# Two more of the seven output sums get a second level of seven-for-eight products, and activations, sums and their results move into rings of one tile

## The chip, the cores and the metric

The kernel runs on one core of a Trainium2 chip. The metric is device time in microseconds (us) of one execution; the kernel before takes 1898.63 us (median of 3 runs, 1898.58 to 1900.76).

## The reference, cut to what matters

```python
def _attn_ref(x):                       # x: (8, 3008, 256) float32
    X = np.fft.fft(x, axis=1)
    X = np.fft.fft(X, axis=2)
    return X.real.astype(np.float32)

def _moe_ref(x, w_in, w_out):           # x: (24064, 256), w_in: (256, 2048), w_out: (2048, 256)
    h = x @ w_in
    g = h * (1.0 / (1.0 + np.exp(-1.702 * h)))
    return (g @ w_out).astype(np.float32)
```

The real part of a two-dimensional Fourier transform of eight sequences, then a layer with 2048 hidden features, a sigmoid-GELU, and a second matrix back to 256 columns. Everything is float32.

## The kernel before, in words

**Stages.** For each of the eight sequences (`b`) the transform over the 3008 positions is done in two stages, 47 x 64 (`fold1`, `mix1`, a round trip through DRAM, `stage2`). The transform over the 256 columns is folded into the first weight matrix (`fold_w`). Position k and its mirror position share the folded operands, so each hidden feature is computed once as a sum (`begin`, two halves `cs`) and the mirrored value is `2*g - x` read backwards (`backward`).

**Steps.** The main loop runs over 384 steps `t`: 8 sequences, 3 blocks `blk`, 2 halves `hh` of 256 (once per sequence 226) positions, and 8 steps `p`, each with two tiles of 128 hidden features. Eight steps with one `(b, blk, hh)` are a group: there are 48, and each gives one pair of output blocks. In a step the activations form a 2 x 2 block matrix, A11 and A12 (forward positions, two feature tiles) and A21 and A22 (mirrored positions).

**First level.** The output of a group is a sum over its eight steps of products of that 2 x 2 matrix with a 2 x 2 matrix of weight tiles. Seven block products with sums of blocks (S1 to S4 of activations, T1 to T4 of weights in `wt`) replace the eight. Each of the seven has its own accumulator in PSUM (`po0` to `po4`, one bank each). A block product is two matmuls of 128 x 64 weights over 256 columns that run side by side in the two halves of the array (`halves`). `product(t)` issues them three steps (`LAG = 3`) after the activations of step t were begun.

**Second level.** For two of the seven, those with A12 and A22 themselves, the operands of two neighbouring steps are cut once more into 2 x 2 and multiplied with seven products of half the width (`small_products`, k = 1 to 7, each one matmul of 64 rows per operand, 128 columns wide). `deeper` makes the four sums that they need, `small_weights` the weight differences. All groups do so but the first (eight plain products) and the last (one level): 46 groups, `deep(t)`.

**End of a group.** `combine` copies the first accumulator out of PSUM (ACT, line 694) and adds others onto it (DVE, line 700). `combine_small`, one step later, puts the small products together (DVE, line 723), `swap` exchanges two halves of the partitions (ACT, lines 731 to 733), `combine_last` adds both levels, transposes and stores.

**Order.** All engines' orders are written out by hand by the loop at the end (a manual schedule); the tile framework adds the waits on semaphores. Within a step PE gets `begin(t, 1)`, part of `product(t-3)`, `begin(t+1)`, the rest of the product, then the small products: k = 1, 2, 4, 7 of the pair that ends in step t-3 in one step, k = 5, 6, 3 in the next. ACT gets `forward` (line 552), `doubled` (545), `activate_back` (559), `middle` (533). DVE gets `backward` (506), two sums of `sums` (574, 575), `deeper` (592). POOL gets the other two sums (571, 572). At the first step of a new group (`t - 3` divisible by 8, called the opening step below) `cut` is 0: PE does `begin(t, 1)` and `begin(t+1)` first, then the product, then the last small products of the old group.

Of the kernel before, what the change touches and what calls it, by code (L numbers as in the profile page):

```python
# [111 lines left out]
def kernel(ctx: ExitStack, tc, x, w_in, w_out, tab1, tab2, out):  # L112
# [12 lines left out]
    hp = ctx.enter_context(tc.tile_pool(name="hp", bufs=4, space=SB))  # L125
    sp = ctx.enter_context(tc.tile_pool(name="sp", bufs=2, space=SB))
# [20 lines left out]

    def mat(w, jj, rows):

        return w[rows, jj * NM:jj * NM + 64]  # L150
# [3 lines left out]
    def bank(name, tag=None):  # L154
        if tag is None:
            tag = spare.pop(0)
            spare.append(tag)
        return psp.tile([128, 512], F32, tag=tag, name=name)
# [198 lines left out]
    def load_in(n, eng):  # L357
        t = raw["in", n] = cv.tile([128, 1024, 2], U32, tag="raw", bufs=3, name="raw")
        eng.dma_start(out=t[:].rearrange("p (i f) w -> p i (f w)", i=2),
                      in_=w_in[:, n * 512:(n + 1) * 512].bitcast(U32).rearrange("(i p) f -> p i f", p=128))  # L360

    def load_out(n, eng):
        t = raw["out", n] = cv.tile([128, 1024, 2], U32, tag="raw", bufs=3, name="raw")
# [5 lines left out]
    def prepare(key):  # L369


        g = sp.tile([128, 1024], F32, tag="s", bufs=3, name="g")
        m = cv.tile([128, 1024], F32, tag="m", bufs=2, name="m")
        r = cv.tile([128, 1024], U32, tag="r", bufs=2, name="r")
        pre[key] = g, m, r
# [28 lines left out]
    def high(key, lo=0, n=1024):  # L404
# [3 lines left out]
        if lo == 0:  # L408
            made_a[key] = cv.tile([128, 1024], U32, tag="a", name="a")
# [57 lines left out]
    vb, ht, st, rt, xb, gt, pot = {}, {}, {}, {}, {}, {}, {}  # L467
    held = []
# [30 lines left out]
    def reversed_sum(t, x, y, op):  # L499

        n, h = width(t), ht[t]
        full, rest = divmod(n, RUN)
        for at, blocks, m in ((0, full, RUN), (full * RUN, 1, rest)):
            if m:
                ins = [free(z[:], at, [256, 2], [RUN, blocks], [1, m]) for z in (x, y)]
                nc.vector.tensor_tensor(free(h[:], 512 + at + m - 1, [256, 2], [RUN, blocks], [-1, m]), *ins, op=op)  # L506

    def rows(t):
# [4 lines left out]
        h = ht[t] = hp.tile([128, 2, 2, 256], F32, tag="h", name="h")  # L513
        dif = sp.tile([128, 512], F32, tag="dif", name="dif")
# [5 lines left out]
        reversed_sum(t, pa, dif, ALU.add)  # L520
# [21 lines left out]
    def doubled(t):  # L542
        n = width(t)
        g = gt[t] = sp.tile([128, 512], F32, tag="dif" if t % 2 else "v", name="g")
        nc.scalar.activation(two(g[:], n), two(xb[t][:], n), ACTF.Copy, scale=2.0)  # L545

    def forward(t):
        n = width(t)
        if t % 2 == 0:
            pot["h"] = cv.tile([128, 2, 2, 2, 256], F32, tag="raw", bufs=3, name="h")  # L550
        h = ht[t] = pot["h"][:, t % 2]
        nc.scalar.activation(two(h[:], n), two(xb[t][:], n), ACTF.Gelu_apprx_sigmoid)  # L552

    def backward(t):
        reversed_sum(t, gt.pop(t), xb.pop(t), ALU.subtract)

    def activate_back(t):
        g = free(ht[t][:], 512, [256, 2], [1, width(t)])
        nc.scalar.activation(g, g, ACTF.Gelu_apprx_sigmoid)  # L559

    def sums(t, eng):
# [3 lines left out]
        h, n = ht[t], width(t)  # L565
        a11, a12, a21, a22 = h[:, 0, 0, :n], h[:, 0, 1, :n], h[:, 1, 0, :n], h[:, 1, 1, :n]
        if eng is nc.gpsimd:
            st[t] = held[2] if t % 4 == 3 else sp.tile([128, 4, 256], F32, tag="s", bufs=3, name="s")
        s1, s2, s3, s4 = (st[t][:, q, :n] for q in range(4))
        if eng is nc.gpsimd:  # L570
            eng.tensor_tensor(s1, a21, a22, op=ALU.add)  # L571
            eng.tensor_tensor(s3, a11, a21, op=ALU.subtract)  # L572
        else:
            eng.tensor_tensor(s2, s1, a11, op=ALU.subtract)  # L574
            eng.tensor_tensor(s4, a12, s2, op=ALU.subtract)  # L575
# [4 lines left out]

    def deeper(t, part):
# [3 lines left out]
        x0, x1, w = ht[t - 1], ht[t], width(t) // 2  # L585
        if part == 0:
            rt[t] = cv.tile([128, 4, 2, 128], F32, tag="r", bufs=2, name="r")
        s1, s2, s3, s4 = (free(rt[t][:], 256 * q, [128, 2], [1, w]) for q in range(4))
        a11, a12, a21, a22 = (free(x[:], 256 + at, [512, 2], [1, w]) for at in (0, w) for x in (x0, x1))
        for out, i0, i1, how in (((s3, a11, a21, ALU.subtract), (s1, a21, a22, ALU.add)),  # L590
                                 ((s2, s1, a11, ALU.subtract), (s4, a12, s2, ALU.subtract)))[part]:
            nc.vector.tensor_tensor(out, i0, i1, op=how)  # L592

    SUBS = {1: (4, 2), 2: (3, 0), 3: (4, 0), 4: (4, 1), 5: (3, 2), 6: (3, 1), 7: (3, 3)}

    def sub(k):
        q, at = SUBS[k]
        return pot[q][:, at * 128:(at + 1) * 128]

    def small_products(t, ks):  # L600
# [4 lines left out]
        if 1 in ks and p == 0:  # L605
            for q in (3, 4):
                pot[q] = bank(f"po{q}", f"o{q}")
        x0, x1, r = ht[t - 1], ht[t], rt[t]
        for k in ks:
            for side in range(2):  # L610
                y0, y1 = (wo[:, p + i, 2, :] if side == 0 else wt[:, p + i, 3, :] for i in range(2))
                made = held[p // 4][:, p // 2 % 2, :, side]
                fwd = {1: (x0, 0), 2: (x1, 0), 4: (x1, w)}
                rhs = (free(fwd[k][0][:], 256 + 512 * side + fwd[k][1], [1, w]) if k in fwd
                       else r[:, {3: 3, 5: 0, 6: 1, 7: 2}[k], side, :w])
                lhs = {1: y0[:, 0:64], 2: y1[:, 0:64], 3: y0[:, 0:0], 4: made[:, 3], 5: made[:, 0], 6: made[:, 1],
                       7: made[:, 2]}[k]
                if k == 3:
                    lhs = y1[:, 64:128]
                nc.tensor.matmul(sub(k)[64 * side:64 * side + 64, :w], lhsT=lhs, rhs=rhs,  # L620
                                 start=(p == 0 and k in (1, 2)), stop=(p == NP - 2), skip_group_check=True)
        if 3 in ks:
            del rt[t]

    def small_weights(n):

        def y(i, at):
            return free(wot[:], (2 * n + i) * 4 * H + 2 * H + at, [NF // 2 * 4 * H + H, 2], [1, 64])

        b11, b12, b21, b22 = y(0, 0), y(0, 64), y(1, 0), y(1, 64)  # L630
        t1, t2, t3, t4 = (held[n // 2][:, n % 2, q] for q in range(4))
        for out, i0, i1 in (t1, b12, b11), (t2, b22, t1), (t3, b22, b12), (t4, b21, t2):
            nc.gpsimd.tensor_tensor(out, i0, i1, op=ALU.subtract)  # L633

    def product(t, lo, hi):

        p, n = steps[t][3], width(t)
        if lo == 0 and p == 0:
            for q in range(2 if t < NP else 3):
                pot[q] = bank(f"po{q}", f"o{q}")  # L640
            if t >= NP and not deep(t):
                pot[5] = bank("po5", "b2" if deep(t - 1) else "o3")
        h = ht[t]
        if t < NP:

            plan = [(half, dh, wo[:, p, 2 * f + dh, :], h[:, half, f, :n])
                    for half in range(2) for dh in range(2) for f in range(2)]
        else:
            s = st[t]
            plan = [(0, 0, wo[:, p, 0, :], h[:, 0, 0, :n]), (0, 1, wt[:, p, 1, :], s[:, 1, :n]),  # L650
                    (1, 0, wt[:, p, 2, :], s[:, 2, :n]), (1, 1, wt[:, p, 0, :], s[:, 0, :n]),
                    (2, 0, wo[:, p, 3, :], s[:, 3, :n])]
# [352 lines left out]
```

## Time and profile before

| | |
|---|---|
| median of 3 runs | 1898.63 us |
| the profiled execution | 1898.94 us, of which the span is 1897.2 us |
| PE (TensorE) busy | 1879.8 us, 99% of the span |
| PEld (weight loads beside the matmuls) | 1364.9 us, 72% |
| DVE / ACT / POOL busy | 1210.5 / 1117.5 / 786.7 us, 64% / 59% / 41% |
| granted TensorE clock | 0.999 |
| DMA | 104.95 MB, 55 GB/s on average |

The profile shows each float32 matmul as two records, so a block product of two matmuls is four records. Records overlap: a product's time is read from the start of one group of records to the start of the next, not from the length of a record.

### The profile page before, as it was taken

Reading aid. Unit: us, or ns where it says so; the run is one execution under the profiler, and the core shown is the slowest. Engines: PE = TensorE matmul, PEld = TensorE weight load, DVE = VectorE, ACT = ScalarE, POOL = GpSimd, SP = SyncE. Lnnn points to the kernel's source line nnn. Section 1 sums busy time; section 2 is a strip of 40 time slices with the busy share of each in tenths; the row PEclk is TensorE's granted clock in tenths of the full one; section 3 lists DMA queues with packets and bytes.
Section 4 is the critical chain, followed back from the end, with each engine's and each line's share of the span. In section 5 each row is a group of like instructions: output and inputs, shape, how many; then the busy total and the mean of one; then the engine's idle time right before and its main releaser. Section 6 shows DMA issues by size and latency. Waiting matters only on the chain.

```text
span 1897.2 us, 51367 instructions
## 1 busy us (share of the span) xinstructions
PE 1879.8 (99%) x21392; PEld 1364.9 (72%) x21392; DVE 1210.5 (64%) x2635; ACT 1117.5 (59%) x2248; POOL 786.7 (41%) x1074
## 2 busy tenths in 40 slices
PE   9999999999999999999999999999999999999998
PEld 6576789777776777777777677777777767777775
DVE  7666556665676556766667556665665766666654
ACT  6656655665556556565565555656655566556553
POOL 4585324633245333462235533365333643223332
PEclk9999999999999999999999999999999999999999
DMA  8732451236221452316413173132720232212201
GB/s 286 165 50 17 102 72 15 48 56 116 18 27 40 77 93 18 51 23 109 57 14 62 22 124 34 24 51 47 114 26 17 18 50 51 24 14 17 29 13 23
DMA packets 145400, 104.95 MB, mean 55 GB/s; under 512 B 104914, under 2 KB 127986, under 8 KB 143984
## 3 DMA queue, kind: packets, MB, share of 16 engines
q1 hardware_dynamic: 143952, 101.14, 32.6%
q8 instruction: 169, 2.77, 0.6%
q10 hardware_dynamic: 1216, 0.52, 0.1%
q14 instruction: 63, 0.52, 0.1%
HBM read 58.38 MB, written 48.01 MB: 56 GB/s over the span
## 4 chain that ended last, share of the span: by engine, by line
PE 93%; POOL 3%; ACT 1%; DVE 1%; DMA 1%; issue 1%; SPq 0%; POOLq 0%; DVEq 0%
PE po L481 42%; PE x L481 33%; PE po L620 14%; PE ps L232 2%; PE ps L334 1%; DMA raw<-in_moe_w_in_dram 1%; POOL wo L444 1%; PE psw L450 1%; ACT xt L235 0%; DMA wo<-in_tab_dram 0%; POOL held L633 0%; POOL wst L426 0%; ACT x L533 0%; POOL s L572 0%; DVE m L412 0%
## 5 line engine op out<-in xcount | busy, mean ns | idle before, releaser
L481 PE MATMUL x<-pq,wcs 128*64 128x256 f32 (+1 forms) x6016 | 765.7, 377 | 1.0 <-ACT x L533 0.2
L506 DVE TENSOR_TENSOR h<-g,x 128x512 f32<-128x512 f32 (+2 forms) x440 | 257.7, 598 | 535.2 <-ACT h L552 534.8
L481 PE MATMUL po<-s,wo 128*64 128x256 f32 (+1 forms) x4512 | 568.6, 375 | 1.3 <-issue 1.3
L481 PEld LDWEIGHTS x<-pq,wcs 128*64 128x64 f32 x6016 | 420.2, 137 | 175.1 <-ACT x L533 18.6
L571 POOL TENSOR_TENSOR s<-h 128x256 f32<-128x256 f32 (+1 forms) x282 | 206.4, 732 | 790.4 <-ACT h L559 771.8
L481 PEld LDWEIGHTS po<-s,wo 128*64 128x64 f32 x4512 | 332.0, 137 | 148.4 <-issue 1.7
L545 ACT ACTIVATE g<-x 128x512 f32<-128x512 f32 (+1 forms) x376 | 222.0, 590 | 341.3 <-PE x L481 340.1
L552 ACT ACTIVATE h<-x 128x512 f32<-128x512 f32 (+1 forms) x376 | 221.4, 589 | 273.2 <-PE x L481 267.8
L533 ACT ACTIVATE x<-nb,af 128x256 f32<-128x256 f32 (+1 forms) x752 | 352.9, 469 | 13.2 <-DVE pq L340 1.0
L481 PE MATMUL po<-h,wo 128*64 128x256 f32 (+1 forms) x1824 | 262.0, 376 | 0.0
L559 ACT ACTIVATE h<-h 128x512 f32<-128x512 f32 (+1 forms) x376 | 231.3, 615 | 32.9 <-DVE h L506 31.7
L572 POOL TENSOR_TENSOR s<-h 128x256 f32<-128x256 f32 (+1 forms) x282 | 205.9, 730 | 0.0
L481 PE MATMUL po<-held,wo 128*64 128x256 f32 (+1 forms) x1504 | 192.4, 375 | 0.0
L571 POOL TENSOR_TENSOR held<-h 128x256 f32<-128x256 f32 (+1 forms) x94 | 76.4, 812 | 257.0 <-ACT h L559 243.5
L620 PE MATMUL po<-r,held 128*64 128x128 f32 (+1 forms) x2208 | 182.9, 270 | 0.0
L481 PEld LDWEIGHTS po<-h,wo 128*64 128x64 f32 x1824 | 133.8, 137 | 60.0
L592 DVE TENSOR_TENSOR r<-h 128x256 f32<-128x256 f32 (+1 forms) x368 | 165.5, 491 | 0.0
L620 PEld LDWEIGHTS po<-r,held 128*64 128x64 f32 x2208 | 141.0, 137 | 23.8
L481 PEld LDWEIGHTS po<-held,wo 128*64 128x64 f32 x1504 | 110.8, 137 | 48.7
L574 DVE TENSOR_TENSOR s<-s,h 128x256 f32<-128x256 f32 (+1 forms) x282 | 127.7, 453 | 0.0
L575 DVE TENSOR_TENSOR s<-h,s 128x256 f32<-128x256 f32 (+1 forms) x282 | 121.0, 429 | 9.6
L620 PE MATMUL po<-h,wo 128*64 128x128 f32 (+1 forms) x1472 | 111.0, 270 | 0.0
(108 smaller groups left out, 1674.4 us busy)
## 6 DMA issues: line engine op xcount, KB each, us to landing
out_dram<-os SPq DMA_DIRECT2D x284, 64.0 KB
Td<-xt SPq DMA_DIRECT2D x14, 768.0 KB
t<-Td SPq DMA_DIRECT2D x7, 1536.0 KB
xt<-in_x_dram SPq DMA_DIRECT2D x14, 512.0 KB
xt<-Xr SPq DMA_DIRECT2D x14, 512.0 KB
nb<-pq SPq DMA_DIRECT2D x23, 256.0 KB
out_dram<-os SPq DMA_DIRECT2D x96, 56.0 KB
Xr<-in_x_dram SPq DMA_DIRECT2D x7, 752.0 KB
```

The source lines that it names most:

```text
L481: nc.tensor.matmul(out[c0:c0 + 64], lhsT=lhs[:, c0:c0 + 64], rhs=rhs, skip_group_check=True, **how)
L506: nc.vector.tensor_tensor(free(h[:], 512 + at + m - 1, [256, 2], [RUN, blocks], [-1, m]), *ins, op=op)
L533: nc.scalar.activation(x[:, i * 256:i * 256 + n], nbt[b, blk][:, hh * 256:hh * 256 + n], ACTF.Copy, scale=af1[:, f:f + 1])
L545: nc.scalar.activation(two(g[:], n), two(xb[t][:], n), ACTF.Copy, scale=2.0)
L552: nc.scalar.activation(two(h[:], n), two(xb[t][:], n), ACTF.Gelu_apprx_sigmoid)
L559: nc.scalar.activation(g, g, ACTF.Gelu_apprx_sigmoid)
L571: eng.tensor_tensor(s1, a21, a22, op=ALU.add)
L572: eng.tensor_tensor(s3, a11, a21, op=ALU.subtract)
L574: eng.tensor_tensor(s2, s1, a11, op=ALU.subtract)
L575: eng.tensor_tensor(s4, a12, s2, op=ALU.subtract)
L592: nc.vector.tensor_tensor(out, i0, i1, op=how)
L620: nc.tensor.matmul(sub(k)[64 * side:64 * side + 64, :w], lhsT=lhs, rhs=rhs, start=(p == 0 and k in (1, 2)), stop=(p == NP - 2), skip_group ...
```

## The change

Four of the seven output sums now go through the second level: A12 and A22 as before, and S4 and S1. Three stay at the first level (A11, S2, S3). The 46 deep groups therefore issue three block products per step instead of five, and per pair of steps 28 small matmuls (four operands, seven products) instead of 14.

So that one DVE operation can serve four operands, the eight blocks of a step lie in one tile `big`: A11, A21, S3, S2 in a ring of four steps (LEFT), and A12, S4, A22, S1 in a ring of three pairs of steps (RIGHT). `deeper` makes its four sums with one operation of 4 x 128 columns each, three of them in one step and the fourth in the next; before, each operation was 2 x 128 wide. `sums` on DVE runs once per pair of steps, 2 x 256 wide, instead of once per step. The rings of the weight preparation (`raw`, `h`, `r`, `m`, `s`, `a`) are places in the same tile.

In PSUM the five accumulator banks become one tile `acc` of 5 x 512 columns. The three plain sums lie in columns 0 to 767, the small products k = 1 in 768 to 1023, the others in 1024 to 2559.

Order: at the opening step PE does the old group's k = 5, 6, 3 right after `begin(t, 1)`, then `begin(t+1)` and the new group's product. In other steps k = 5, 6, 3 stand ahead of the product's last part. `combine_small` stands ahead of the sums, and `combine_last` and the transposes are spread over three steps. `small_weights` moves from POOL (16 operations) to DVE (32, for four operands). In the prologue the load of the last quarter of `w_in` is issued after the second read of `Td`, which moves ahead of it, and `high(out0)` moves up.

```diff
-    hp = ctx.enter_context(tc.tile_pool(name="hp", bufs=4, space=SB))
+    acc = psp.tile([128, 5 * 512], F32, tag="acc", name="acc")
+    big = cv.tile([128, 19 * 1024], F32, tag="big", name="big")
...
+        if tag[0] == "o":
+            return acc[:, int(tag[1]) * 512:(int(tag[1]) + 1) * 512]
...
+    LEFT, RIGHT, MADE, SUM, RES, OUT = 0, 4096, 10240, 14336, 16384, 18432
+    A11, A21, S3, S2 = range(4)
+    A12, S4, A22, S1 = range(4)
...
     def sums(t, eng):
...
+        if t % 2 == 0:
+            return
+        a11, s2 = (free(big[:], at_left(t - 1, q), [1024, 2], [1, n]) for q in (A11, S2))
+        a12, s4, s1 = (free(big[:], at_right(t - 1, q), [1024, 2], [1, n]) for q in (A12, S4, S1))
+        eng.tensor_tensor(s2, s1, a11, op=ALU.subtract)
+        eng.tensor_tensor(s4, a12, s2, op=ALU.subtract)
...
+    def raws(t, half):
+        return free(big[:], at_right(t, 0) + half * (width(t) // 2), [256, 4], [1, width(t) // 2])
+    def made_sum(q, w):
+        return free(big[:], SUM + 512 * q, [128, 4], [1, w])
     def deeper(t, part):
...
-        for out, i0, i1, how in (((s3, a11, a21, ALU.subtract), (s1, a21, a22, ALU.add)),
-                                 ((s2, s1, a11, ALU.subtract), (s4, a12, s2, ALU.subtract)))[part]:
+        s1, s2, s3, s4 = (made_sum(q, width(t) // 2) for q in range(4))
+        a11, a12, a21, a22 = (raws(k, half) for half in range(2) for k in (t - 1, t))
+        for out, i0, i1, how in (((s3, a11, a21, ALU.subtract), (s1, a21, a22, ALU.add), (s2, s1, a11, ALU.subtract)),
+                                 ((s4, a12, s2, ALU.subtract),))[part]:
...
+    SPOT = {2: 0, 6: 1, 5: 2, 7: 3, 3: 4, 4: 5}
+    def spot(pair_, k):
+        return 768 + 128 * pair_ if k == 1 else 1024 + 768 * pair_ + 128 * SPOT[k]
+    def both(k, *dims):
+        return free(acc[:], spot(0, k), [spot(1, k) - spot(0, k), 2], *dims)
     def small_products(t, ks):
...
+            for pr in range(2):
+                for side in range(2):
+                    op_ = 2 * pr + side
+                    weights, q = ((wo, 2), (wo, 3), (wt, 3), (wt, 0))[op_]
...
     def product(t, lo, hi):
...
-            plan = [(0, 0, wo[:, p, 0, :], h[:, 0, 0, :n]), (0, 1, wt[:, p, 1, :], s[:, 1, :n]),
-                    (1, 0, wt[:, p, 2, :], s[:, 2, :n]), (1, 1, wt[:, p, 0, :], s[:, 0, :n]),
-                    (2, 0, wo[:, p, 3, :], s[:, 3, :n])]
+            plan = [(0, 0, wo[:, p, 0, :], left(t, A11, n)), (0, 1, wt[:, p, 1, :], left(t, S2, n)),
+                    (1, 0, wt[:, p, 2, :], left(t, S3, n))]
...
     def combine(t):
...
+        nc.scalar.copy(c11, acc[:, 0:n])
+        nc.vector.tensor_tensor(c12, c11, acc[:, 256:256 + n], op=ALU.add)
+        nc.vector.tensor_tensor(c21, c12, acc[:, 512:512 + n], op=ALU.add)
         if deep(t):
+            nc.scalar.copy(free(big[:], RES + 1024 + 384, [512, 2], [1, w]), both(1, [1, w]))
+            return
...
     def combine_small(t):
...
+        for out, i0, i1 in ((res(0, 1024), res(1024 + 384, 0), both(2, [128, 2], [1, w])),
+                            (res(1024 + 128, 128), res(1024, 0), both(5, [128, 2], [1, w])),
+                            (res(256, w - 256), res(1024 + 128, 128), both(3, [128, 2], [1, w])),
+                            (res(256 + w), res(1024 + 256), both(5, [1, w]))):
             nc.vector.tensor_tensor(out, i0, i1, op=ALU.add)
...
+            opening = (t - LAG) % NP == 0 and t >= NP + LAG
+            one, other = (t - LAG, (1, 2, 4, 7)), (t - LAG - 1, (5, 6, 3))
+            if opening:
+                small_products(*other)
+            cut = 0 if opening and not after else 3 if after else 2
             product(t - LAG, 0, cut)
...
+            if not opening:
+                small_products(other[0], other[1][after:])
+            product(t - LAG, cut, 6 if t - LAG == last else None)
+            small_products(one[0], one[1][after:])
             swap(t - LAG - 2)
...
+            combine_small(t - LAG - 1)
...
+            sums(t - 1, nc.vector)
             deeper(t - 2, 0)
             deeper(t - 3, 1)
```

In the built program, engine by engine, each wait names the semaphore count that it waits for, and so the instruction that ends it. Around the end of each of the 46 deep groups it has these waits. The copy of c11 (ACT) waits for the last small matmul of the group's last step (k = 7). The adds c12 and c21 (DVE) follow it, and the copy of the k = 1 results (ACT) waits for c21. The first k = 5 matmul of the opening step (PE) waits for that copy. The first operation of `combine_small` (DVE) waits for the last matmul of the new group's first product, and the first matmul of the new group's second product (PE) waits for the last operation of `combine_small`. In the last of the 46 it is the seventh product of the opening step that waits so.

## The prediction

> **What bounds the kernel now.** I read the page's parts 1, 2 and 4 first.
>
> ```profile
> span 1897.2 us, 51367 instructions
> PE 1879.8 (99%) x21392; PEld 1364.9 (72%) x21392; DVE 1210.5 (64%) x2635; ACT 1117.5 (59%) x2248; POOL 786.7 (41%) x1074
> PEclk9999999999999999999999999999999999999999
> PE 93%; POOL 3%; ACT 1%; DVE 1%; DMA 1%; issue 1%; SPq 0%; POOLq 0%; DVEq 0%
> ```
>
> PE is busy in every slice at full clock, and the chain of waits is 93% PE. Matmul time taken off PE comes off the total, and any wait that PE gets is added in full: nothing lies beside it. So I read the timeline around one group's end, where the new accumulators are opened. The opening step starts at 986.45 us. PE, ACT and DVE (start us, length us, engine, line, operation; idle time before it in brackets):
>
> ```profile
> 986.23 0.39 PE L620 MATMUL po<-r,held 128*64 128x128 f32 x4
> 986.45 1.90 PE L481 MATMUL x<-pq,wcs 128*64 128x256 f32 x16
> 986.49 0.36 ACT L694 COPY u<-po 128x256 f32<-128x256 f32 x1
> 986.89 0.95 DVE L700 TENSOR_TENSOR u<-u,po 128x256 f32<-128x256 f32 x2 [1.15 <-ACT u L694]
> 987.53 0.60 ACT L552 ACTIVATE h<-x 128x512 f32<-128x512 f32 x1 [0.52 <-PE x L481]
> 987.87 0.69 DVE L700 TENSOR_TENSOR c<-u,po 128x512 f32<-128x512 f32 x1
> 988.18 0.60 PE L481 MATMUL po<-h,wo 128*64 128x256 f32 x4
> 988.61 1.90 PE L481 MATMUL po<-s,wo 128*64 128x256 f32 x16
> 988.66 0.42 DVE L700 TENSOR_TENSOR c<-c,po 128x256 f32<-128x256 f32 x1
> 990.34 0.61 PE L620 MATMUL po<-r,held 128*64 128x128 f32 x8
> 990.77 0.39 PE L620 MATMUL po<-r,wo 128*64 128x128 f32 x4
> 990.99 1.03 PE L481 MATMUL x<-pq,wcs 128*64 128x256 f32 x8
> 991.60 1.58 DVE L723 TENSOR_TENSOR held<-held,po 128x256 f32<-128x256 f32 x4
> 991.86 0.60 PE L481 MATMUL po<-h,wo 128*64 128x256 f32 x4
> 992.13 0.60 ACT L552 ACTIVATE h<-x 128x512 f32<-128x512 f32 x1 [0.92 <-PE x L481]
> ```
>
> The reader is to see three things. Starts give the prices on PE: four records of 256 columns (one block product) take 988.61 - 988.18 = 0.43 us, eight records of 128 columns 990.77 - 990.34 = 0.43, so a pair of small matmuls costs 0.22, and `begin` 0.87 (990.99 to 991.86). PE has no gap at the group's end. And the copy (986.49) starts before the last small matmuls have ended (986.23 + 0.39 = 986.62), so it doesn't wait for them: in this kernel each accumulator bank is a tile of its own, and `combine` runs beside PE.
>
> **Part 1: matmuls.** Per pair of steps, two operands leave the first level: 2 x 2 block products of 0.433 (12 records from 1002.88 to 1004.18 are three products in 1.30) go, 4 x 0.433 = 1.73 us; 14 small matmuls come, 7 x 0.2175 = 1.52. The gain is 0.21 us. At width 226, `begin` takes 0.76 (1009.49 to 1010.25), a product 0.38 and a small pair, by half, 0.19: gain 0.19. 46 deep groups have 184 pairs, 32 of them (8 sequences x 4) 226 wide: 152 x 0.21 + 32 x 0.19 = 38.0 us less. It is all on the path. Weight loads double in number for these products, but at 128 columns the old ones already keep exactly half the time of 256, so loads do not limit them.
>
> **Part 2: the first new wait.** `acc` is one tile now, and the built program orders every reader and writer of it one after the other, whatever columns they touch. Take T as the start of an opening step. The copy of c11 waits for the last k = 7 matmul, then the chain runs through DVE and ACT back to PE's first k = 5 matmul. Row by row: PE to ACT 0.27 (`begin` issued by 991.86, ACT L552 starts 992.13), with rounding 0.28; copy 0.36; to DVE 0.04 (986.85 to 986.89); two dependent adds 0.98 (986.89 to 987.87); to ACT 0.03 (DVE's `backward` ends 989.68, ACT's L559 starts 989.71); copy of the k = 1 results, now 2 x 128 columns, 0.36; to PE 0.05 (ACT's L533 ends 1017.92, PE's `begin` starts 1017.97). That is T + 2.1 less rounding, 2.07 with T + 0.28 as the start of the copy. PE's cover is `begin(t, 1)`, 0.87. Exposed: 1.20 us, 46 times: 55.2 us. Bounds: 0.98 if the two adds follow at DVE's undependent spacing (0.34 + 0.42), 1.5 if `middle` (0.98 us on ACT just ahead of the copy, ended about 986.55) is 0.3 late. ACT's `forward` is queued behind the second copy, 0.9 us later than now; behind it `backward` and POOL's sums, whose results PE wants three steps later.
>
> **Part 3: the second new wait.** `combine_small` waits for the new group's first product, and PE's next product waits for `combine_small`. Counted from the end of that product: PE to DVE 0.28 (as for ACT); three operations of 512 columns and one of 256, each but the last needing the one before: the row at 987.87 to 988.66 gives 0.79 for 512 dependent from PSUM, `combine_last` to transpose (995.29 to 996.01) 0.72; I take 0.75, so 2.25 + 0.42; to PE 0.14 (in the chain DVE ends 79.42, PE starts 79.56). Sum 3.09. Cover: `begin(t+1, 1)`, 0.87. Exposed 2.22. In 14 of the 46, a `mix1` stands there too (seven sequences, two each): the chain gives line 232 1.6% of the span for 28 of them, 1.08 us; the timeline at 124.01 to 124.81 gives 0.80; I take 1.0, exposed 1.22. The last of the 46 has no `begin` between: 3.09. Together 31 x 2.22 + 14 x 1.22 + 3.1 = 89.0 us. Bounds: 1.77 with undependent spacing (0.60 per 512), which makes 68; 2.8 if POOL beside it slows DVE by the fifth that line 592's mean (509 ns) stands over its median (417), which makes 116.
>
> **Part 4: costed at nothing.** DVE per pair of steps: now eight operations of 0.42 at lines 574, 575 and 592, 3.4 us; then six of 0.69 (the 128x512 row), 4.1. The 184 x 0.7 = 129 us lie in the 535 us in which line 506 waits for ACT. The longer work after an opening (`combine_small`, three `deeper`, `backward`) ends S2 at about T + 12 us where PE wants it at about T + 14; with that cover gone it is rival C. ACT's three swaps (0.40 to 0.59, the 128x512 copy row) and copy add 0.7 us per group, beside PE. Prologue: POOL loses 16 operations of line 633 (about 7.5 us) just ahead of the one larger PE gap below, a gain of at most 1.8; DVE gets 32 of them at 0.28 (its 128x128 row), 9 us over four steps, and the `w_in` quarter loads later, behind a read of `Td` on SP's queue; its first user is step 2's weight preparation. A loss of 3 at most, by PE's gaps there (0.2 to 0.6 us each). I take zero. POOL's S1 and S3 keep their number and size.
>
> The one gap of the old main loop that resembles the new ones, and the clock around it:
>
> ```profile
> 124.01 0.44 PE L232 MATMUL ps<-xt,w 47*64 47x256 f32 x3 [1.78 <-POOL xt L208]
> 122.00:126.00 4.00, 2.22 (x28) 1.28 (x24) 0.69 (x1) 1.03 (x3) 3.92 (x7) 1.00 0.00 0
> ```
>
> The granted clock (the 1.00 after the five engines) stays full over a gap of 1.78 us, so I keep full-clock prices.
>
> A rule against the change: the Trainium skill, "TensorE: Matmul & The Clock Gate", section "What's actually happening", has PE fall to half clock after an idle window of about 3.4 us. The gaps of 1.2 and 2.2 us stay under it; if it struck at each second wait and held for one window, 46 x 1.7 = 78 us would be added, about 2083. A rule for it: "PSUM — Partial Sum Buffer", section "PSUM bank collisions raise a hardware error", asks for waits by bank (or bank and quadrant), not by address; the copy at 986.49 beside matmuls into another bank agrees. By that rule neither wait of parts 2 and 3 is needed, and the sum is 1861; the built program has both, so I go by the program.
>
> **Sum.** The profiled execution took 1898.94 us, 0.3 over the median. 1898.9 - 38.0 + 55.2 + 89.0 = 2005.1 us: slower by 5.6%.
>
> **Rivals.** A: the waits end early enough to be hidden. Place: the two waits at the opening; price 144 us less, 1861 us, faster by 2%. For it: PE has no gap there now. Against: the two chains contain eight operations whose rows exist, and 0.87 us of cover. It decides where both together fall under 38.0 / 46 = 0.83 us per group. B: one of the two is hidden, for instance because work that I don't see stands between on PE: 1916 to 1950. Against: the order on PE is fixed and has only `begin` there. C: the gaps spread. DVE's backlog makes S2 late, or a cold clock follows: up to 1 us more per group, 46 to 80 us, 2050 to 2085. For it: only about 2 us of slack in S2; against: line 506's idle time. D: the change doesn't do what it says, the small matmuls costing more than half: excluded by the 0.43 of eight records.
>
> **Numbers.** Forecast 0.83, A 0.06, B 0.05, C 0.06. The forecast's own bounds: 1898.9 - 38.0 + 46 x 0.98 + 68 - 1.8 = 1972, and 1898.9 - 38.0 + 69 + 116 + 3 = 2049. The range 1968 to 2046 leaves out A, B and C. A measurement tells about 0.2% (4 us) from no change. Faster 0.06, same 0.01 (between A and B), slower 0.93.
>
> **What would show it.** PE busy near 1842 us in a span near 2003. Among the waits, PE for ACT's copy of the k = 1 results 46 times, 1.2 us each, and PE for DVE's `combine_small` 46 times, about 2 us each; PE without gaps between openings; clock 1.0. If there is no gap at the openings, parts 2 and 3 are wrong. If gaps come in each step, it is DVE or the `big` tile (rival C). A saving in PE's busy time other than 38 us would make part 1 wrong.

## The result and the profile after

The changed kernel takes 2033.42 us (median of 4 runs, 2031.64 to 2034.38), the kernel before 1899.64 (4 runs, 1898.58 to 1900.76): a ratio of 1.070, 95% interval 1.069 to 1.072. The forecast was 2005.0 with a range of 1968 to 2046. The profiled execution took 2034.38 us, 135.4 more than the one before. From the page of the changed kernel, parts 1, 2 and 4:

```profile
span 2032.6 us, 55416 instructions
PE 1881.3 (93%) x23600; PEld 1409.7 (69%) x23600; DVE 1493.0 (73%) x2245; ACT 1154.4 (57%) x2248; POOL 934.2 (46%) x1058
...
PEclk9899999999999999999999999999999999999999
...
PE 83%; DVE 9%; ACT 6%; issue 1%; DMA 1%; POOL 0%; SPq 0%; ACTq 0%; DVEq 0%; POOLq 0%
```

PE was busy in 99% of the span and is now busy in 93%. The chain that ended last, 93% PE before, now runs through DVE for 9% and through ACT for 6%: PE waits for them. In these slices the clock is full but for the beginning. The view of the waits of PE (line waited at, and by whose work the wait ended: us in total, times, longest):

```profile
PE acc L493 <- DVE big L758: 61.2, 44, 1.8
PE acc L657 <- ACT big L731: 45.8, 46, 2.0
PE acc L493 <- DVE dif L549: 5.1, 2, 2.8
```

The first two are the two waits that the prediction's parts 2 and 3 priced; line 758 is `combine_small`, line 731 the copy of the k = 1 results. These totals count idle time after the modelled ends of the matmuls; what a wait adds is read from starts. The timeline at one opening step (start us, length us; idle time in brackets):

```profile
1026.14 1.03 PE L493 MATMUL x<-pq,wcs 128*64 128x256 f32 x8
1026.36 0.37 ACT L726 COPY big<-acc 128x256 f32<-128x256 f32 x1
1026.76 0.42 DVE L727 TENSOR_TENSOR big<-big,acc 128x256 f32<-128x256 f32 x1 [0.93 <-ACT big L726]
1027.22 0.42 DVE L728 TENSOR_TENSOR big<-big,acc 128x256 f32<-128x256 f32 x1
1027.67 0.37 ACT L731 COPY big<-acc 128x256 f32<-128x256 f32 x1 [0.94 <-DVE big L728]
1028.10 1.09 PE L657 MATMUL acc<-big 128*64 128x128 f32 x16 [0.92 <-ACT big L731]
...
1031.62 1.03 PE L493 MATMUL x<-pq,wcs 128*64 128x256 f32 x8
1031.83 2.46 DVE L758 TENSOR_TENSOR big<-big,acc 128x512 f32<-128x512 f32 x4 [2.57 <-PE acc L493]
...
1034.35 1.08 PE L493 MATMUL acc<-big,wo 128*64 128x256 f32 x8 [1.70 <-DVE big L758]
```

`begin` keeps PE for 0.86 us (eight records of 107.9 ns). The first one, from 1026.14, would be followed at 1027.00; the small matmuls start at 1028.10, so 1.10 us are exposed. They wait for copy, add, add, copy, one after the other on ACT and DVE, as the prediction chained them. The second `begin`, from 1031.62, covers to 1032.48, and the next product starts at 1034.35: 1.87 us exposed, behind the four operations of `combine_small`.

The third wait above is none of the openings. The start of ACT's first `combine` copy marks the end of the first group with a second level (called the first group below): 138.46 us in the kernel before (first line), 169.98 after (second line).

```profile
138.46 0.34 ACT L694 COPY u<-po 128x226 f32<-128x226 f32 x1
169.98 0.34 ACT L726 COPY big<-acc 128x226 f32<-128x226 f32 x1
```

Thus 31.5 of the 135.4 us come before the main loop has properly begun. From the last such copy to the end are 8.7 us, before 10.2. Between the first and the last one lie 1748.5 us before and 1853.9 after: 105.3 more for 46 groups. The window from 40 to 60 us of this beginning (its length, busy us of the five engines with their instructions, granted clock, DMA share, GB/s), first before the change, then after:

```profile
40.00:60.00 20.00, 19.18 (x140) 11.15 (x138) 17.87 (x25) 16.60 (x24) 10.65 (x7) 1.00 1.01 348
40.00:60.00 20.00, 15.10 (x65) 7.71 (x63) 10.19 (x15) 11.59 (x17) 6.37 (x6) 0.74 0.73 251
```

The clock was 0.74 and not 1.00, and PE had 65 matmul records there, against 140 before. Its timeline there:

```profile
48.29 1.97 PE L493 MATMUL acc<-pq,wcs 128*64 128x256 f32 x8 [2.27 <-DVE dif L549]
...
60.19 3.22 PE L493 MATMUL acc<-pq,wcs 128*64 128x256 f32 x16 [2.81 <-DVE dif L549]
```

These are `begin`-like products of the prologue, into `acc`: `bank()` hands pieces of the one tile to the prologue too. PE waits for DVE to finish reading the last piece, and the eight records take the time from 48.29 to 50.02, 1.73 us, twice the 0.86 of the main loop: half clock.

### The profile page after: what moved, and what is told of

Read it like the earlier page. It is cut to its first block, busy times and chain, and to the rows that moved or that the text cites. A ratio compares the mean times of both kernels' runs of the same rounds, so it can differ in the third digit from the quotient of the medians.

```text
span 2032.6 us, 55416 instructions
## 1 busy us (share of the span) xinstructions
PE 1881.3 (93%) x23600; PEld 1409.7 (69%) x23600; DVE 1493.0 (73%) x2245; ACT 1154.4 (57%) x2248; POOL 934.2 (46%) x1058
## 4 chain that ended last, share of the span: by engine, by line
PE 83%; DVE 9%; ACT 6%; issue 1%; DMA 1%; POOL 0%; SPq 0%; ACTq 0%; DVEq 0%; POOLq 0%
PE x L493 27%; PE acc L657 26%; PE acc L493 25%; DVE big L758 5%; PE ps L346 1%; DVE big L728 1%; DVE big L727 1%; ACT big L731 1%; PE ps L244 1%; ACT x L564 1%; ACT xt L247 1%; ACT big L726 1%; ACT big L579 1%; DVE big L623 1%; DVE big L602 0%
## 5 line engine op out<-in xcount | busy, mean ns | idle before, releaser
L594 POOL TENSOR_TENSOR big<-big 128x256 f32<-128x256 f32 (+1 forms) x376 | 353.1, 939 | 1005.5 <-ACT big L586 770.6
L493 PE MATMUL acc<-big,wo 128*64 128x256 f32 (+1 forms) x4832 | 631.0, 377 | 66.3 <-DVE big L758 61.2
L623 DVE TENSOR_TENSOR big<-big 128x512 f32<-128x512 f32 (+1 forms) x736 | 609.5, 844 | 34.6 <-PE acc L657 19.8
L493 PEld LDWEIGHTS acc<-big,wo 128*64 128x64 f32 x4832 | 340.7, 137 | 231.9 <-DVE big L758 81.0
L537 DVE TENSOR_TENSOR big<-g,x 128x512 f32<-128x512 f32 (+2 forms) x440 | 255.4, 592 | 239.5 <-ACT big L579 238.6
L657 PE MATMUL acc<-big 128*64 128x128 f32 (+1 forms) x5888 | 385.8, 272 | 47.4 <-ACT big L731 45.8
L657 PEld LDWEIGHTS acc<-big 128*64 128x64 f32 x5888 | 334.1, 137 | 90.5 <-ACT big L731 66.4
L579 ACT ACTIVATE big<-x 128x512 f32<-128x512 f32 (+1 forms) x376 | 221.4, 589 | 216.7 <-PE x L493 182.7
L595 POOL TENSOR_TENSOR big<-big 128x256 f32<-128x256 f32 (+1 forms) x376 | 341.5, 908 | 0.0
L657 PE MATMUL acc<-big,wo 128*64 128x128 f32 (+1 forms) x4416 | 303.9, 271 | 0.0
L657 PEld LDWEIGHTS acc<-big,wo 128*64 128x64 f32 x4416 | 259.4, 137 | 28.1
L586 ACT ACTIVATE big<-big 128x512 f32<-128x512 f32 (+1 forms) x376 | 231.8, 616 | 30.3 <-DVE big L537 28.9
L602 DVE TENSOR_TENSOR big<-big 128x512 f32<-128x512 f32 (+1 forms) x188 | 140.2, 746 | 6.5
L601 DVE TENSOR_TENSOR big<-big 128x512 f32<-128x512 f32 (+1 forms) x188 | 131.8, 701 | 1.5 <-POOL big L594 1.5
```

The lines of the kernel that those rows point to most:

```text
L493: nc.tensor.matmul(out[c0:c0 + 64], lhsT=lhs[:, c0:c0 + 64], rhs=rhs, skip_group_check=True, **how)
L537: nc.vector.tensor_tensor(free(out, at + m - 1, [by, 2], [RUN, blocks], [-1, m]), *ins, op=op)
L579: nc.scalar.activation(front(t), two(xb[t][:], width(t)), ACTF.Gelu_apprx_sigmoid)
L586: nc.scalar.activation(back(t), back(t), ACTF.Gelu_apprx_sigmoid)
L594: eng.tensor_tensor(right(t, S1, n), left(t, A21, n), right(t, A22, n), op=ALU.add)
L595: eng.tensor_tensor(left(t, S3, n), left(t, A11, n), left(t, A21, n), op=ALU.subtract)
```

## The experiments

My theory after the result had three parts. (1) The tile `acc` as such makes the waits, by joining five banks into one thing to be ordered, in the openings and in the prologue alike. (2) The waits of the openings add to PE's time in full. (3) Without them the matmuls give their 38 us. The rivals: the second level's longer DVE and ACT work makes PE late in any case; the prologue is slower because of its other edits (moved loads, weight differences on DVE). Each experiment kernel computes the whole result.

**The prologue alone.** Five separate bank tiles until step `t = NP + LAG`, the joined tile from there on:

```diff
-    acc = psp.tile([128, 5 * 512], F32, tag="acc", name="acc")
+    acc = None
+    old = early_banks.enter_context(tc.tile_pool(name="old", bufs=1, space=PS))
...
+        if tag[0] == "o" and acc is None:
+            return old.tile([128, 512], F32, tag=tag, name=name)
...
+        if t == NP + LAG:
+            early_banks.close()
+            acc = psq.tile([128, 5 * 512], F32, tag="acc", name="acc")
```

> The changed kernel, but up to the end of the first group the five accumulator banks are five tiles; only from then on are they the one tile acc. Theory 1 (all of the loss is waits that exist because acc is one tile: 31 us of it in the prologue, the rest at the 46 openings): the first c11 copy, at 170.0 us in the changed kernel and 138.5 in the one before, comes back to 138 to 141 us, and the time is 2033 - 31 = 2002 us (1998 to 2007), with 46 waits of about 1.1 and 1.9 us left. Rival (the prologue lost its 31 us to the rest of the change: loads in another order, 32 small weight differences on DVE, rings in one tile): the first c11 copy stays later than 155 us and the time above 2018.

Measured: 2003.52 us (1999.67 to 2008.04), ratio 1.054 (1.053 to 1.056). The first group ends at 144.07 us instead of 169.98, and the main stretch is 1853.5 us, as in the changed kernel. Its wait for `combine_small` in the same view:

```profile
PE acc L497 <- DVE big L762: 61.2, 44, 1.8
```

It is the same to 0.1 us in total, and so is the one for the k = 1 copy (45.7 us, 46 times). So the joined tile cost the prologue some 26 us, and it is this kernel, joined in the main loop only, that my sum of 2005 describes.

**Two tiles.** Banks 0 and 1 in one tile, 2 to 4 in another, so that neither wait of the openings remains:

```diff
-    acc = psp.tile([128, 5 * 512], F32, tag="acc", name="acc")
+    acc = psp.tile([128, 2 * 512], F32, tag="acc", name="acc")
+    acs = psp.tile([128, 3 * 512], F32, tag="acs", name="acs")
```

> The changed kernel with acc cut into two tiles, banks 0 and 1 (plain sums and k = 1) and banks 2 to 4 (the other small products). Theory 1: both waits at the openings are gone, 2033 - 142 = 1891 us, less what the prologue gets back from having two groups of banks instead of one: 1870 to 1893. Rival (the openings wait for other reasons: the length of ACT's and DVE's chain, whatever the tiles are): PE still has gaps there, and the time stays above 1950.

Measured: 1909.27 us (1907.23 to 1914.68), ratio 1.004 (1.003 to 1.006), between the theory's range and the rival's. The waits for `combine_small` and for the k = 1 copy are gone, and the main stretch falls from 1853.9 to 1738.0 us. But the prologue ends at 166.1 us: there three banks are still one tile (PE waits 6.2 us there for line 551, the same operation as line 549 above). And four of the 46 intervals are 1.0 to 6.0 us longer than in the next kernel, 12.4 us together. One of these has a wait of 0.9 us for `middle`; the last one has no pause, only a later c11 copy. The two longest, 9.6 us together, have pauses of 1.9 and 3.1 us that end with no wait that the profile names, each with half clock beside it (granted clock 0.50 from 1120 to 1124 us). The longest pause:

```profile
1119.61 1.12 PE L662 MATMUL acs<-big,wo 128*64 128x128 f32 x8 [3.14 <-issue]
1120.42 2.02 PE L495 MATMUL x<-pq,wcs 128*64 128x256 f32 x8
```

What caused these two stays open. Shorter pauses of this kind (1.1 to 1.9 us) stand once or a few times in the kernel before and in the next one too.

**Five tiles.** Each bank its own tile, as in the kernel before, and the small products placed so that each operation of `combine_small` reads one bank:

```diff
-    acc = psp.tile([128, 5 * 512], F32, tag="acc", name="acc")
+    accs = [psp.tile([128, 512], F32, tag=f"acc{i}", name=f"acc{i}") for i in range(5)]
...
-        return 768 + 128 * pair_ if k == 1 else 1024 + 768 * pair_ + 128 * SPOT[k]
+        return 256 + 128 * pair_ if k == 1 else 256 * pair_ + 128 * (SPOT[k] % 2)
+    def room_of(k):
+        return accs[1 if k == 1 else 2 + SPOT[k] // 2]
```

> The changed kernel with five accumulator tiles, one per bank; the small products are laid so that each combine operation reads one bank only. Theory 1: prologue as before the change and no waits at the openings: 1898.9 - 38.0 = 1861 us (1857 to 1868). Rival (the second level of two more sums, its wider DVE sums or the pairwise order cost PE time themselves): above 1875, with waits of PE for DVE inside the groups.

Measured: 1880.51 us (1878.68 to 1881.56), ratio 0.990 (0.988 to 0.991). From its page:

```profile
PE 1855.9 (99%) x23600; PEld 1419.1 (75%) x23600; DVE 1510.7 (80%) x2245; ACT 1152.7 (61%) x2248; POOL 952.6 (51%) x1058
```

PE is busy in 99% again with the longer DVE work all there, so the changed kernel's loss does not come from the length of that work. The change's arithmetic, without its one tile, makes the kernel faster by 1.1%. But the time is 19.5 us above the 1861 expected and inside the rival's range (above 1875), so theory (3) fell: the main stretch is 1726.0 us, a gain of 22.5 and not of 38, and the first group ends at 143.5, 5.1 us later than before. 2.1 of these 5.1 are the arrival of the first table (ACT's first operation on it starts at 10.76 us, in the profiled run before at 8.68; over the kernels here it differs from 8.3 to 10.8).

**The one tile without the rest of the change.** The kernel before, with nothing changed but that `bank()` cuts its five accumulators from one tile:

```diff
+    acc = psp.tile([128, 5 * 512], F32, tag="acc", name="acc")
...
+        if tag[0] == "o":
+            return acc[:, int(tag[1]) * 512:(int(tag[1]) + 1) * 512]
```

> The kernel before, with one edit: its five accumulator banks are one tile. No product, sum or order is changed. Theory 1: the prologue loses about 31 us; at an opening PE waits for the copy and four DVE operations after two begins (0.28 + 0.36 + 0.04 + 0.98 + 0.79 + 0.42 + 0.14 - 1.73 = 1.3 us) and for combine_small (0.28 + 1.58 + 0.14 - 0.87 = 1.1 us), less some 0.9 us in 14 of 46: 1899 + 31 + 98 = about 2028 us (2010 to 2045). Rival (the loss belongs to the new products, sums and rings): 1899 to 1910 us.

Measured: 2023.16 us (2020.28 to 2028.78), ratio 1.065 (1.063 to 1.067). Three lines make the old kernel 123 us slower. The view of PE's waits:

```profile
PE acc L484 <- ACT held L706: 52.5, 46, 1.3
PE acc L484 <- DVE held L726: 24.7, 32, 0.9
```

The same two places, in a kernel with none of the change's other edits; the first group ends at 172.2 us. Together with the five tiles this shows theory (1) from both sides.

**Where the rest of the 38 us went, first pair.** In steps that carry a `mix1` or a `stage2`, the five-tile kernel has small waits of PE for ACT; and near 108 to 111 us a gap of 2.2 us. One edit for each:

```diff
-            if t < n:
-                forward(t)
             if after and t + 1 < n:
                 middle(t + 1)
+            if t < n:
+                forward(t)
```

> The kernel with five separate bank tiles, with one order changed: in the steps that carry a mix1 or a second stage, ACT now issues the copies of the previous step's second half ahead of the activations of the next step, as it does in plain steps. Theory (the waits of 0.55 and 0.22 us that PE has in those steps come from ACT's order): PE's idle time in those steps goes; 28 such steps by 0.3 to 0.5 us is 8 to 14 us, so 1866 to 1873 us, and the 226-wide groups fall from 37.35 us to below 37.0. Rival (those waits come from elsewhere, or the activations that now stand second become the late ones): no gain, 1876 to 1886 us.

```diff
-        at(8 + i, small_weights, i)
+        at(8 + 2 * i, small_weights, i)
```

> The kernel with five separate bank tiles, with one placing changed: DVE's eight blocks of weight differences come in every second step from step 8 on, not in every step. Theory (about 3 us of the prologue are PE's wait, around 105 to 111 us of the run, for a reversed sum that stands behind these 32 operations on DVE): the first group ends about 3 us earlier, near 141 us instead of 143.5, and the time is 1876 to 1879 us. Rival (the wait there has another cause, such as the arrival of the first tables, which differs from run to run): 1879 to 1883 us and the same wait in the trace.

And both edits in one kernel:

> The kernel with five separate bank tiles and both edits: the copies ahead of the activations in the special steps, and the weight differences in every second step. Theory: the two gains add, 1863 to 1871 us, faster than the kernel before by 1.5 to 1.9%. Rival (neither wait is where it was seen): within 4 us of the five-tile kernel, 1877 to 1885 us.

Measured: 1878.50 us (1877.04 to 1882.28), 1880.29 (1879.86 to 1884.26) and 1880.20 (1878.44 to 1881.00), ratios 0.989, 0.990 and 0.989, each within 0.002. All three times lie in their rivals' ranges. With the copies ahead, the groups with a `mix1` fall from 40.15 to 40.02 us, but the 226-wide groups go from 37.35 to 37.40, and the waits for ACT's line 576 grow from 2.2 to 3.9 us in all: the wait moved. With the differences spread out, the later waits of 0.35 and 0.30 us at 116.90 and 117.80 us disappear, but new ones of 1.03 and 1.33 us for `middle` come at 119.22 and 129.03, and the gap of 2.2 us stays, because its cause is the first block of eight, which is where it was (the kernel with the differences on POOL, below, shows the cause). On DVE these eight stood from 105.11 to 108.64 us ahead of `backward`: while POOL's four operations of line 453 ran, the first took 0.41 us and the next three 0.77 to 0.82; after that the last four took 0.28 to 0.29.

**Second pair.** ACT's swap behind `activate_back` instead of ahead of `backward`, and the weight differences on POOL, where they were before the change:

```diff
-            swap(t - LAG - 2)
             if t < n:
                 backward(t)
...
                 activate_back(t)
                 sums(t, nc.gpsimd)
+            swap(t - LAG - 2)
```

> The kernel with five separate bank tiles, with one order changed: ACT's three copies of the partition swap (0.62 us each) stand behind doubled and activate_back, not ahead of them. Theory (where a special step follows an opening, the three copies hold up ACT's g, whose read frees the tile that PE's begin writes: 6 waits, 2.2 us in all, and in the 226-wide groups what eats the gain): the six waits of PE for ACT's g go, the 226-wide groups fall from 37.35 us by 0.3 or more, and the time is 1876 to 1879 us. Rival (another operation of ACT, the half-second copies of the special step, is then the late one): the waits stay at over 1.5 us in total, 1879 to 1882 us.

Measured: 1928.04 us (1926.97 to 1930.16), ratio 1.015 (1.014 to 1.016): my theory fell, and so did its rival. A plain group takes 37.69 us instead of 36.55. The timeline of one:

```profile
507.73 0.62 ACT L769 COPY big<-big 64x512 f32<-64x512 f32 x1
...
509.66 0.99 ACT L564 ACTIVATE x<-nb,af 128x256 f32<-128x256 f32 x2
510.70 1.08 PE L493 MATMUL x<-pq,wcs 128*64 128x256 f32 x8 [1.07 <-ACT x L564]
```

The three copies now stand right ahead of `middle`, whose result `begin` is added to, and PE waits 1.07 us. The six waits for line 576, 2.2 us in all, are no longer in the view, and 50 waits for `middle`, 50.3 us in all, are there instead. ACT is busy in 60% of the span, and still only one of the two places tried is cheap.

```diff
-                nc.vector.tensor_tensor(out, i0, i1, op=ALU.subtract)
+                nc.gpsimd.tensor_tensor(out, i0, i1, op=ALU.subtract)
...
-        at(8 + i, small_weights, i)
+        at(max(7 + i, 8), small_weights, i)
```

> The kernel with five separate bank tiles, with the 32 weight differences back on POOL instead of DVE, at the steps at which the kernel before has its 16. Theory (PE's gap of 2.2 us near 108 to 111 us comes from DVE's first eight differences, which take up to 0.8 us each beside POOL and hold up a reversed sum): this gap goes, and the first group's end, counted from the start of ACT's first operation on the first table (132.8 us in the five-tile kernel, 129.8 in the kernel before), comes to 130 to 131 us; the time 1877 to 1879 us. Rival (32 operations of 0.46 us, 15 us on POOL, make POOL's sums S1 and S3 late instead): a new wait of PE for POOL or DVE of the same size, no gain, 1880 to 1884 us.

Measured: 1886.70 us (1885.64 to 1890.97), ratio 0.993 (0.992 to 0.995): slower than with the differences on DVE, as the rival said, and by more. The gap of 2.2 us is gone, and the timeline has this one instead:

```profile
118.89 1.07 DVE L601 TENSOR_TENSOR big<-big 128x452 f32<-128x452 f32 x1 [10.18 <-POOL big L594]
...
120.02 1.02 PE L493 MATMUL acc<-big,wo 128*64 128x226 f32 x4 [8.56 <-DVE big L601]
```

POOL had eight differences and four operations of line 453 ahead of S1, DVE waited 10 us for S1, and PE for DVE. The change's move of the differences to DVE is thus worth its 2.2 us: with twice as many of them, POOL's queue is the worse place.

> The kernel with five separate bank tiles and three edits together: the copies of the next half ahead of the activations in special steps, the swap behind activate_back, the weight differences on POOL. Theory: the gains add up, 1871 to 1876 us, faster than the kernel before by 1.2 to 1.5%. Rival (each edit only moves its wait): 1878 to 1883 us.

Measured: 1928.43 us (1927.37 to 1930.85), ratio 1.015 (1.014 to 1.017). It is far outside both expectations, because it contains both bad edits; its waits are 47.1 us for `middle` and 8.5 us once for line 601. Of all versions, the five tiles as they are, with the copies ahead, with the differences spread out or with both are the fastest: 1878.5 to 1880.5 us, not told apart by their intervals, 1.1% under the kernel before and 7.5% under the changed one.

## Why the prediction was right, and which step failed

The total came out 28 us over the forecast, in the upper part of a range that was made for the sizes of two waits. That it also held a third loss, which the sum had at nothing, is luck. The terms, from the two profiled spans and the five-tile kernel:

| step | predicted, us | measured, us |
|---|---|---|
| part 1, matmuls, all on the path (measured with five tiles, their small waits included) | -38.0 | -22.5 |
| parts 2 and 3, two waits at 46 openings | +144.2 | +127.8 |
| part 4, prologue | 0 (at most +3) | +31.5 |
| after the last group | 0 | -1.4 |
| sum on the profiled span | +106.2 | +135.4 |

**What bounds the kernel** held: PE at 99%, any wait added in full. The main stretch grew by 105.3 us where the terms for it gave 106.2; but that agreement is of two errors that cancel.

**Part 1 was too high by 15.5 us. Its prices were nearly right; the step that failed is "It is all on the path".** A plain group of four pairs of steps takes 37.19 us before and 36.55 with five tiles: 0.16 us a pair, not 0.21. A pair has 72 records of 256 columns and 28 of 128 in the old kernel, 56 and 56 in the new. By the starts (medians over both kernels after 400 us) a record of 256 columns takes 107.9 ns and one of 128 takes 54.6, a little over half. A block product then costs 0.432 us and a pair of small matmuls 0.218, within 0.002 us of what I took. At these prices the old group has 37.19 us, as measured, and the new one 36.39: a gain of 0.20 us a pair. The other 0.16 us of the group are a wait that the five tiles leave. From the timeline of a plain group:

```profile
426.44 1.22 DVE L743 TENSOR_TENSOR big<-big 128x512 f32<-128x512 f32 x1
...
427.76 0.96 DVE L779 TENSOR_TENSOR big<-big 128x768 f32<-128x768 f32 x1
...
428.63 0.68 DVE L537 TENSOR_TENSOR big<-g,x 128x512 f32<-128x512 f32 x1
...
429.35 0.63 ACT L586 ACTIVATE big<-big 128x512 f32<-128x512 f32 x1 [1.13 <-DVE big L537]
429.89 0.97 ACT L564 ACTIVATE x<-nb,af 128x256 f32<-128x256 f32 x2
429.94 1.03 PE L493 MATMUL acc<-big,wo 128*64 128x256 f32 x8
...
430.91 1.08 PE L493 MATMUL x<-pq,wcs 128*64 128x256 f32 x8
```

On DVE `backward` (line 537) stands behind `combine_last` (lines 743 and 779). ACT's line 586 waits for `backward`, `middle` (line 564) stands behind that, and PE's `begin` is added to the result of `middle`. The eight records from 429.94 take 0.86 us; `begin` starts at 430.91, 0.11 us later than that, and its own eight records take 0.91 us, 0.05 more than usual. In the old kernel no record of such a group starts late. Part 4 had this longer work at a group's end "beside PE"; it is not quite.

At the rows' prices all 184 pairs would have given some 36 us, so about 13 of the 15.5 us do not come from the prices. Besides the 0.16 us of the plain groups, these parts are seen. In the 226-wide groups, 37.38 us before and 37.35 with five tiles, 0.7 us were due (382 ns a product, 193 ns a small pair), and PE's waits take most of it back. In six of the eight it is the one for ACT's line 576, 0.54 us from start to start, right behind ACT's three swap copies (part 4 costed the swaps at nothing "beside PE"; with the swaps moved, these six waits were gone, though others came). In the last one it is 0.7 us for `middle`. And the first interval of the main stretch takes 42.79 us and not 40.67, with waits of 0.8 us for DVE and 0.7 us for ACT that the old kernel does not have there; the rest of it is not separated. Where else to put the swaps wasn't found. The sign that the prediction set against its own part 1 did come: PE's busy time is 1881.3 us and not near 1842, and with five tiles it is 23.9 us less than before and not 38.

**Part 2**: 1.20 us predicted, 1.10 at the opening shown. The chain is as described, each hand-over a few hundredths shorter. **Part 3**: 2.22 predicted, 1.87 there. The four dependent operations took 2.46 us and not 2.67, the two hand-overs 0.27 and not 0.42. Both waits are there 46 and 44 times, at the lines named. Against the five tiles, plain groups lose 2.92 us, nearly the full 2.97 of the two waits, so theory (2) holds; the 226-wide ones, where `mix1` covers more, lose 0.9. Together the 46 openings cost 127.8 us: 1853.9 less 1726.0.

**Part 4 is the step that failed most**, and less in the longer work of DVE and ACT (above) than in the prologue. It reads: "Prologue: [...] I take zero", with 3 us as the upper bound. I looked there for what the moved weight differences and loads cost, and found part of it: DVE's first eight differences do make a gap of 2.2 us. But the prologue's own matmuls also get their PSUM from `bank()`, and the edit to `bank()` makes one tile of five for every caller. The rule that I applied to the openings in parts 2 and 3 ("orders every reader and writer of it one after the other, whatever columns they touch") I did not apply to the callers before the main loop. The kernel that joins the tile in the main loop only takes 29.9 us less than the changed one, which shows it: 25.9 of the 31.5 us are its. Of the 5.6 that stay with the joined tile put in late, 1.0 is the later arrival of the first table in that run; the gap of 2.2 us, a wait of 2.0 us for DVE's line 605 at 116.21 and half clock right after it (granted clock 0.50) are the likely rest, not separated further. The profile of before had the sign of what was at stake: PE busy for 97.4 of the 100 us from 20 to 120 us.

**The rivals.** A and B, hidden waits: fell, one wait is in all 46 openings and the other in 44. C: fell as a cost of each group, because PE's waits of over 0.4 us in the main loop are at the openings but for three (0.7, 1.6 and 2.8 us). Its cold clock came in the prologue and at two openings (granted clock 0.50 from 174 to 176 and from 304 to 306 us), not after. D: fell.

**The two rules.** The clock rule of the Trainium skill ("TensorE: Matmul & The Clock Gate", "What's actually happening") was weighed at 78 us more, should it strike at each second wait. It struck at two of the 46 openings, both before 310 us; from 400 to 2000 us the granted clock of the changed kernel is 1.00, so the gaps of 1.1 and 1.9 us there did not bring it down, and keeping full price was nearly right. By the rule of "PSUM — Partial Sum Buffer", "PSUM bank collisions raise a hardware error", waits go by bank, which gave 1861 us. The built kernel's waits go by tile, as the program showed; where tiles are banks the measured time is 1880.5.

## What to carry to other kernels

Merging buffers into one tile, to let one instruction span them, also merges their waits: before doing it, list every place that gets a piece of the new tile, set-up code included, and ask for each reader which writer it now holds up. Here the waits cost about 150 us and the joined tile saved no operation (DVE has 2245 with one tile and with five); one tile per bank, with the operands laid out so that each operation stays inside a bank, kept the gain of the arithmetic. When a gain is the difference of two large sums of matmul time, price one matmul from the starts of long runs of records, and hold a group's time against that price: what is left over is waiting, here about a third of the gain. Before moving work on an engine that is idle 40% of the time look at what stands right behind it in that engine's queue.

## What the runs showed of the hardware

The granted clock fell after shorter gaps than I expected, and not each time. The five-tile kernel's windows after PE's gap of 2.2 us (which ends at 110.82):

```profile
110.00:112.00 2.00, 1.18 (x8) 0.79 (x10) 1.97 (x3) 1.20 (x3) 1.98 (x3) 0.73 0.46 84
112.00:114.00 2.00, 2.00 (x18) 1.60 (x16) 1.93 (x6) 0.55 (x1) 1.92 (x5) 0.50 0.65 121
```

And the kernel with the copies ahead, after a gap of 2.28 us at the same place (which ends at 108.40):

```profile
110.00:112.00 2.00, 2.00 (x38) 1.81 (x36) 1.97 (x5) 0.04 (x1) 1.92 (x5) 1.00 0.56 150
```

In the two microseconds that begin 1.2 and 1.6 us after the gap's end the clock is 0.50 in the one (its second line) and 1.00 in the other, for gaps that differ by 0.1 us. Half clock also came with the gaps of 2.27 and 2.81 us in the changed kernel's prologue and with the pause of 3.14 us above, where `begin` took 1.71 us and not 0.86. In the main loop of the changed kernel it came at the opening at 172.75 us, after a gap of 2.0 us, and at the one at 303.21, where a pause of 1.6 us and the opening's 0.9 us stand close together. The 44 other openings, with gaps of up to 1.9 us, show none, nor does a single pause of 2.75 us at 1184.77 (clock 1.00 from 1185 to 1195). The Trainium skill ("TensorE: Matmul & The Clock Gate", "What's actually happening") names an idle window of about 3.4 us that runs free of the program. That it is free of the program agrees with the two windows above; but gaps of 2.0 to 3.1 us were enough here, so a gap need not fill 3.4 us, and a wait of 2 us can cost another 1 to 2 us of slow matmuls.

Small DVE operations slowed beside POOL: of the differences of 128 x 128, three of the four that ran while POOL's line 453 did took 0.77 to 0.82 us, and the four after it 0.28 to 0.29 us.
